# Thirteen warm-up products for eleven, and the state space parameters in nine transfers for five

## The chip, the core and the metric

The kernel runs on one core of a Trainium2 chip. The metric is device time in microseconds (us): the median of the runs of one kernel. A profile is one further execution under the hardware profiler; its times count from the first instruction of the program, and its span ends with the last. Names of engines: PE is TensorE (PEld are its weight loads, and in the profile also its waits and branches), ACT is ScalarE, DVE is VectorE, POOL is GpSimd, SP is SyncE, which issues most DMA transfers.

## The reference, cut to what matters

```python
x = A_u                                  # 1 x 2048 x 640, float32
xn = layernorm(x)                        # over the 640 features
K = 2.0 * einsum("dn,dnl->dl", C * dt, exp(A * dt * pos)).real      # 640 x 128 modes
y = irfft(rfft(xn.T, 2 * L) * rfft(K, 2 * L))[:, :L].T + xn * D_skip
h = xn @ w1 + b1                         # 640 -> 1728
act = h * tanh(softplus(h))              # mish
return x + y + act @ w2                  # 1728 -> 640
```

A normalisation, a state space layer (a long convolution for each feature) and a dense layer with mish, all three added to the input.

## The kernel before, in words

The 2048 rows are worked on in four blocks of 512 (`NB`, `TB`). PE does the dense layer: for each block and each of 14 chunks of the 1728 hidden features (`FC`), a first product (15 matmuls of 512 columns at L807, or 30 of 256 at L800 for the chunk of 64, or the five parts of `mm1_pair` at L827 in later blocks) and, three chunks later, a second product into five accumulators (L859). Each operand is split into a high and a low float16 part, which is why a product takes three matmuls. ACT and DVE compute mish between the two products (L890 to L926), split the weights (L552 to L562) and do the state space layer, which for the parameters of this input comes down to running sums (`skip_a` to `skip_e`). A test on the device, `flag`, says whether these shortcuts hold; if not, a general version is run behind the main one (`ffn_general`, `ssm_general`). That version is part of the program, so at the end each engine that has code in it jumps over it.

The order of the work is set by hand for the first block (the string `ORDER`, L1251) and by a planner (`Plan`) from then on. In the first part:

- `fill(n)` (L1244) gives PE n float32 products of the identity with itself (L1246) while the first rows are on their way. They write `tr`, and nobody reads the result. In the trace, one such product is two weight loads and two matmuls.
- `to_t0` (L1236) transposes the normalised rows on PE; the rows come from `norm0_a` (ACT, L1224) and `norm0` (DVE, L1221).
- `load_par` (L657) is called by the planner once, as the operation `("lp",)` (L1147). SP issues there one transfer after another at L661: `log_A_real`, `A_imag` and `C_real` whole, `C_imag` in two pieces. Behind it stand on SP the five transfers of `load_xt` (L1209) and then the loads of further weights (L543, L538). The parameters are read from L671 on (ACT), L674 (DVE).

Eight completion counters (`DMAHW0` to `DMAHW7` in the listings below) are handed out in turn to the transfers that SP and ACT issue. A transfer waits, before it is issued, until the earlier transfer with the same counter has landed. At the end of the program SP waits for all counters one after the other, and then all five engines meet twice (L1344 in the profile): POOL collects the others, lets them go, clears the semaphores, collects them again and lets them go again.

The last piece of the work is `tail` (L1078): the last accumulators are drained (`drain`, L931) and stored by SP (L934).

Of the kernel before, what the change touches and what calls it, by code (L numbers as in the profile page):

```python
# [28 lines left out]
KD = D // P  # L29
# [423 lines left out]
def body(ctx: ExitStack, tc: tile.TileContext, x, xT, logA, Aim, Cr, Ci, logdt, vec, w1, w1T, w2, w2T, out):  # L453
# [79 lines left out]
    def load_w1(f, queues=(sp,)):  # L533
        t = kf(pl["w1", f])
        n, m = FC[f], P // len(queues)
        for j, e in enumerate(queues):
            o = D * FO[f] + j * m * KD * n
            e.dma_start(t[j * m:(j + 1) * m, :, :n], w1[o:o + m * KD * n].rearrange("(p k f) -> p k f", p=m, k=KD))  # L538

    def load_w2(f):  # L540
        t = pl["w2", f]
        n = FC[f]
        sp.dma_start(t[:n], w2[FO[f]:FO[f] + n])  # L543
        if n < P:
            sp.dma_start(t[n:2 * n], w2[FO[f]:FO[f] + n])
# [111 lines left out]
    def load_par():  # L657
        t = big.tile([P, 4, KD, NS], F32, name="par", tag="bigB")
        for j, src in enumerate((logA, Aim, Cr, Ci)):
            for k in (slice(0, KD),) if j < 3 else (slice(0, 3), slice(3, KD)):  # L660
                sp.dma_start(t[:, j, k], src.rearrange("(k p) n -> p k n", p=P)[:, k])  # L661
        return t

# [272 lines left out]
    def whole():  # L936
# [208 lines left out]


        add(("lp",), S, 0.4, lambda: SM.update(par=load_par()), rel=start(0, 4), kb=1310.0)  # L1147
        ops = list(mode_ops())
        last = {e: ("lp",) for e in (A, V)}
# [94 lines left out]
    def fill(n):  # L1244
        for _ in range(n):
            pe.matmul(TR[:, 0:P], ident, ident, start=True, stop=True)  # L1246
# [24 lines left out]
    def products(s):  # L1271
        f, k, half = int(s[0]), int(s[-2]), s[-1]
        kinds = [s[i:i + 2] for i in range(1, len(s) - 2, 2)]
        start = (f, half) not in count
        count[f, half] = count.get((f, half), 0) + len(kinds)
        mm1_part(f, kinds, CA if half == "a" else CB, start=start, stop=count[f, half] == 3 * KD, ks=[k])

    with tc.manual_schedule():

        for i in range(2):  # L1280
            sp.dma_start(X0[:, i, 0:320], xr[0, i, :, 0:320])
            a.dma_start(X0[:, i, 320:D], xr[0, i, :, 320:D])
        a.activation(warm, one, AF.Sigmoid)
        for f in range(6):
            pl.take("w", ("w1", f))
            if f < 2:
                pl.take("w", ("w2", f))
        for i in range(2):
            load_w1(i)
            sp.dma_start(X0[:, i + 2], xr[0, i + 2])  # L1290
        load_w1(2)
        sp.dma_start(cv[:, 0:24], vec)
        load_w1(3)
        load_w2(0)
        load_w1(4)
        load_w2(1)
        load_w1(5)
        fill(11)
        S, count = {}, {}
        act = {"S": statistics, "M": moments, "N": norm0, "A": norm0_a, "T": to_t0, "H": hi_w1, "L": lo_w1}  # L1300
        row = {"h": hi0, "l": lo0}
        for s in ORDER.split():
            if s[0].isdigit():
                products(s)
            elif s[0] in row:
                row[s[0]](int(s[1]), CA if s[2] == "a" else CB)
            else:
                act[s[0]](int(s[1]))
        a.activation(bs, cv[:, 0:NF], AF.Copy, scale=SH)
# [38 lines left out]
```

## Time and profile before

| | us |
|---|---|
| median of 3 runs (lowest, highest) | 360.02 (360.0, 360.07) |
| the profiled execution, its own time | 359.66 |
| span of the profiled execution | 357.9 |
| PE busy | 350.5 (98%) |
| DVE busy | 305.9 (85%) |
| ACT busy | 295.3 (83%) |
| POOL busy | 48.8 (14%) |

Busy time is a share of the span. An engine's instructions that only wait, branch or issue a DMA are not counted as busy; the profile lists them apart, with a q behind the engine's name.

### The profile page before, as it was taken

How to read it: one execution, taken by the hardware profiler on the slowest of the kernel's cores; microseconds unless marked ns; L12 is line 12 of the kernel's file. 1: busy time of each engine (PE TensorE's matmuls, PEld its weight loads, DVE VectorE, ACT ScalarE, POOL GpSimd, SP SyncE). 2: the span in 40 equal slices, each digit the busy share in tenths (PEclk: the TensorE clock that was granted, in tenths of full speed). 3: DMA queues.
4: the chain of work that ended last, by engine and by line, in shares of the span. 5: the costliest groups of instructions: out<-in, count | busy, mean ns of one | idle time of the engine just before them, and what ended most of it. 6: DMA issues, size and time to landing. Idle time of an engine off the chain costs nothing.

```text
span 357.9 us, 6182 instructions
## 1 busy us (share of the span) xinstructions
PE 350.5 (98%) x2253; PEld 215.5 (60%) x2253; DVE 305.9 (85%) x583; ACT 295.3 (83%) x620; POOL 48.8 (14%) x74
## 2 busy tenths in 40 slices
PE   7999999999999999999999999999999999999994
PEld 7754444444666666665666666666566666566542
DVE  5989989989999999999999877899988788885452
ACT  4699999977588699989899887989989978958630
POOL 2200000000023221000004341000002361000000
PEclk9999999999999999999999999999999999999999
DMA  7869975303819926900536963922002895121012
GB/s 262 327 175 287 323 220 159 93 0 79 289 43 166 284 69 169 326 31 14 144 126 122 271 175 75 326 76 66 2 0 30 137 219 118 23 37 31 2 57 96
DMA packets 25988, 48.75 MB, mean 136 GB/s; under 512 B 3528, under 2 KB 6880, under 8 KB 25952
## 3 DMA queue, kind: packets, MB, share of 16 engines
q1 hardware_dynamic: 19424, 34.86, 30.2%
q0 software_dynamic: 6240, 13.11, 18.6%
q8 instruction: 19, 0.31, 0.4%
q10 hardware_dynamic: 288, 0.33, 0.3%
q14 instruction: 17, 0.14, 0.1%
HBM read 39.10 MB, written 5.26 MB: 124 GB/s over the span
## 4 chain that ended last, share of the span: by engine, by line
PE 96%; DVE 1%; DMA 1%; ACT 0%; issue 0%
PE acc L859 48%; PE h L827 18%; PE h L807 12%; PE tr L827 12%; PE h L800 2%; PE h L789 2%; PE tr L789 1%; DMA x<-in_A_u_dram 1%; PE acc L1236 0%; DVE st L627 0%; DVE st L628 0%; ACT x L1224 0%; PE acc L873 0%; PE acc L870 0%; PE acc L871 0%; DVE w1l L556 0%
## 5 line engine op out<-in xcount | busy, mean ns | idle before, releaser
L859 PE MATMUL acc<-hi,w2h 128*128 128x512 f16 x273 | 100.9, 379 | 0.0
L859 PE MATMUL acc<-hi,w2l 128*128 128x512 f16 (+1 forms) x265 | 99.7, 379 | 0.0
L859 PE MATMUL acc<-lo,w2h 128*128 128x512 f16 x253 | 93.3, 379 | 0.0
L859 PEld LDWEIGHTS <-w2h 128*128 128x128 f16 x526 | 50.9, 98 | 48.3 <-issue 1.9
L890 ACT ACTIVATE s<-h,cv 128x512 f32<-128x512 f32 (+1 forms) x55 | 32.7, 594 | 29.0 <-PE h L827 23.4
L827 PEld LDWEIGHTS <-w1h 128*128 128x128 f16 x432 | 42.3, 98 | 10.6
L910 DVE SCALAR_TENSOR_TENSOR A<-p,A 128x512 f32<-128x512 f32 (+1 forms) x56 | 37.0, 661 | 8.5 <-ACT p L906 8.1
L859 PEld LDWEIGHTS <-w2l 128*128 128x128 f16 x273 | 25.6, 98 | 30.7 <-issue 1.1
L926 DVE SCALAR_TENSOR_TENSOR lo<-A,hi 128x512 f16<-128x512 f32 x52 | 35.5, 682 | 8.0 <-ACT hi L916 8.0
L894 DVE SCALAR_TENSOR_TENSOR A<-h,bs,s 128x512 f32<-128x512 f32 (+1 forms) x55 | 34.8, 636 | 6.4 <-ACT s L890 6.4
L898 ACT ACTIVATE p<-s,kc 128x512 f32<-128x512 f32 (+1 forms) x56 | 39.3, 701 | 0.6
L902 ACT ACTIVATE p<-p,kc 128x512 f32<-128x512 f32 (+1 forms) x56 | 39.3, 702 | 0.5
L906 ACT ACTIVATE p<-p,kc 128x512 f32<-128x512 f32 (+1 forms) x56 | 39.2, 700 | 0.4
L916 ACT ACTIVATE hi<-A 128x512 f16<-128x512 f32 x52 | 32.4, 623 | 2.6 <-DVE A L910 2.5
L548 POOL DMA_DIRECT2D r<-in_xT_dram x15 | 13.4, 1000 | 134.2 <-DVE r L768 66.3
L749 DVE TENSOR_TENSOR_SCAN g<-g,car,kc 128x512 f32<-128x512 f32 x20 | 25.6, 1278 | 1.7 <-ACT g L743 1.6
L827 PEld LDWEIGHTS <-w1l 128*128 128x128 f16 x216 | 21.1, 98 | 8.2
L753 DVE TENSOR_TENSOR_SCAN g<-g,car,g 128x512 f32<-128x512 f32 x20 | 25.5, 1276 | 0.0
L827 PE MATMUL tr<-xh,w1l 128*128 128x256 f16 x90 | 24.5, 273 | 0.0
L827 PE MATMUL tr<-xh,w1h 128*128 128x256 f16 x90 | 24.5, 273 | 0.0
L827 PE MATMUL tr<-xl,w1h 128*128 128x256 f16 x90 | 24.5, 273 | 0.0
L827 PEld LDWEIGHTS <-swh 128*128 128x128 f16 x216 | 21.1, 98 | 4.4
(177 smaller groups left out, 726.6 us busy)
## 6 DMA issues: line engine op xcount, KB each, us to landing
w<-in_w_dram SPq DMA_DIRECT2D x25, 320.0 KB, 5.1
x<-in_A_u_dram SPq DMA_DIRECT2D x14, 320.0 KB, 4.3
w<-in_w2T_dram SPq DMA_DIRECT2D x15, 288.0 KB, 6.8
w<-in_B_w_dram SPq DMA_DIRECT2D x13, 320.0 KB, 3.5
w<-in_w1T_dram SPq DMA_DIRECT2D x13, 320.0 KB, 6.5
xt<-in_xT_dram SPq DMA_DIRECT2D x15, 256.0 KB, 5.9
r<-in_xT_dram POOLq DMA_DIRECT2D x15, 256.0 KB, 6.1
xt<-r POOLq DMA_DIRECT2D x15, 256.0 KB, 4.7
```

Of the source, the lines that this page charges most:

```text
L749: v.tensor_tensor_scan(g1[:, 1:], g1[:, 1:], zero.to_broadcast([P, TB]), car[:, 1, k:k + 1], op0=OP.add, op1=OP.add)
L807: pe.matmul(o, w, x, start=(j == 0), stop=(j == len(order) - 1))
L827: pe.matmul(o, p, q, start=start and n == 1, stop=n == 3 * len(w), skip_group_check=True)
L859: pe.matmul(o, w, x, start=start, stop=stop)
L890: a.activation(pl["s", b, f][:, c], bank(b, f)[:, c] if h is None else h, AF.Sigmoid, bias=cv[:, f:f + 1], scale=1 / SH)
L894: v.scalar_tensor_tensor(pl["A", b, f][:, c], bank(b, f)[:, c] if h is None else h, bs[:, f:f + 1], pl["s", b, f][:, c], op0=OP.add, op1=O ...
L898: a.activation(pl["p", b, f][:, cols(f)], pl["s", b, f][:, cols(f)], AF.Arctan, bias=one, scale=-1.0)
L902: a.activation(p, p, AF.Square, bias=pi4, scale=2.0)
L906: a.activation(p, p, AF.Tanh, bias=mb, scale=MG)
L910: v.scalar_tensor_tensor(A, pl["p", b, f][:, cols(f)], MC, A, op0=OP.add, op1=OP.mult)
L916: a.activation(hi, A, AF.Copy, scale=MA * SA / SH)
L926: v.scalar_tensor_tensor(lo, A, MA * SA / SH, hi, op0=OP.mult, op1=OP.subtract)
```

## The change

`fill` is called with 13 for 11, and `load_par` splits each of the first three parameters into the first three and the last two groups of 128 features, and `C_imag` into two, two and one.

```diff
@@ load_par
         for j, src in enumerate((logA, Aim, Cr, Ci)):
-            for k in (slice(0, KD),) if j < 3 else (slice(0, 3), slice(3, KD)):
+            for k in ((slice(0, 3), slice(3, KD)) if j < 3 else (slice(0, 2), slice(2, 4), slice(4, KD))):
                 sp.dma_start(t[:, j, k], src.rearrange("(k p) n -> p k n", p=P)[:, k])
@@ the first part
         load_w1(5)
-        fill(11)
+        fill(13)
```

On PE, the start of the program, before (-) and now (+): `tr` is where the warm-up products go, `acc` where the transposes go.

```order
 L1344 UNCONDITIONAL_BRANCH
-L1246 MATMUL tr<-ident 128x128 x11
+L1246 MATMUL tr<-ident 128x128 x13
 L1236 MATMUL acc_216<-ident,x_257 128x128
 L1236 MATMUL acc_214<-ident,x_257 128x128 x2
```

Two products more stand ahead of the first transpose; everything behind them on PE stands in the same order, two products (eight instructions in the trace) later in the program.

On SP, around the load of the parameters (`par`), before; the counter in brackets is the one that the transfer takes itself, and `xt` is the block of rows for the second block.

```order
L538 DMA w_226<-in_w_dram 128x640 [waits DVE_49]
L661 DMA par<-in_A_log_A_real_dram 128x5x128 [waits DMAHW2_49]
L661 DMA par<-in_A_A_imag_dram 128x5x128 [waits DMAHW3_49]
L661 DMA par<-in_A_C_real_dram 128x5x128 [waits DMAHW4_49]
L661 DMA par<-in_A_C_imag_dram 128x3x128 [waits DMAHW5_49]
L661 DMA par<-in_A_C_imag_dram 128x2x128 [waits DMAHW6_49]
L1209 DMA xt<-in_xT_dram 128x512 [waits DMAHW7_49]
```

The same place now:

```order
L538 DMA w_226<-in_w_dram 128x640 [waits DVE_49]
L661 DMA par<-in_A_log_A_real_dram 128x3x128 [waits DMAHW2_49]
L661 DMA par<-in_A_log_A_real_dram 128x2x128 [waits DMAHW3_49]
L661 DMA par<-in_A_A_imag_dram 128x3x128 [waits DMAHW4_49]
L661 DMA par<-in_A_A_imag_dram 128x2x128 [waits DMAHW5_49]
L661 DMA par<-in_A_C_real_dram 128x3x128 [waits DMAHW6_49]
L661 DMA par<-in_A_C_real_dram 128x2x128 [waits DMAHW7_49]
L661 DMA par<-in_A_C_imag_dram 128x2x128 [waits DMAHW0_49]
L661 DMA par<-in_A_C_imag_dram 128x2x128 [waits DMAHW1_49]
L661 DMA par<-in_A_C_imag_dram 128x128 [waits DMAHW2_49]
L1209 DMA xt<-in_xT_dram 128x512 [waits DMAHW3_49]
```

Four transfers more stand there, so every transfer behind them takes the counter four further on.

On SP, the six stores at the end of the program (`tail`), before:

```order
L934 DMA out_dram<-xt 128x512 [waits DMAHW6_49,DVE_49]
L934 DMA out_dram<-xt 128x512 [waits DMAHW7_49,DVE_49]
L934 DMA out_dram<-xt 128x512 [waits DMAHW0_49,DVE_49]
L934 DMA out_dram<-xt 128x512 [waits DMAHW1_49,DVE_49]
L934 DMA out_dram<-xt 128x256 [waits DMAHW2_49,DVE_49]
L934 DMA out_dram<-xt 128x256 [waits DMAHW3_49,DVE_49]
L1321 COMPARE_AND_BRANCH
```

And now:

```order
L934 DMA out_dram<-xt 128x512 [waits DMAHW2_49,DVE_49]
L934 DMA out_dram<-xt 128x512 [waits DMAHW3_49,DVE_49]
L934 DMA out_dram<-xt 128x512 [waits DMAHW4_49,DVE_49]
L934 DMA out_dram<-xt 128x512 [waits DMAHW5_49,DVE_49]
L934 DMA out_dram<-xt 128x256 [waits DMAHW6_49,DVE_49]
L934 DMA out_dram<-xt 128x256 [waits DMAHW7_49,DVE_49]
L1321 COMPARE_AND_BRANCH
```

The stores are the same; the last of them took counter 3 and takes counter 7 now, the last of the eight. `L1321` is the jump over the general version.

## The prediction

> **What bounds the kernel now.** I read the page first, then the waits of PE, then the end of the span, where the busy times say nothing. From the page:
>
> ```profile
> span 357.9 us, 6182 instructions
> PE 350.5 (98%) x2253; PEld 215.5 (60%) x2253; DVE 305.9 (85%) x583; ACT 295.3 (83%) x620; POOL 48.8 (14%) x74
> ```
>
> The waits of PE over the whole span (who waited for whom: sum in us, times, longest):
>
> ```profile
> PE tr L1246 <- POOL ident masks.py:199: 1.5, 1, 1.5
> PE acc L1236 <- ACT x L1224: 0.5, 1, 0.5
> ```
>
> PE waits twice, at the very start, and never again: behind the head, the time is a fixed stream of matmuls. So three places can move the time: the head (until PE has its rows), a new wait in the stream, and what comes behind the last matmul. PE is busy for 350.5 us and starts at 1.5; that leaves some 5 us behind it. They are not empty. The last store (issue and landing), the jump over the general version, and the first instructions of the end (L1344):
>
> ```profile
> L934 SPq DMA_DIRECT2D out_dram<-xt x1: 332/332/332, 353.1 to 353.1; - x1
> DMA to landing us min/median/max: 2.0/2.0/2.0
> ```
>
> ```profile
> L1321 PEldq COMPARE_BRANCH  x1: 3874/3874/3874, 350.5 to 350.5; - x1
> ...
> L1321 PEldq EVENT_SEMAPHORE  x1: 51/51/51, 354.4 to 354.4; - x1
> ```
>
> ```profile
> L1344 SPq EVENT_SEMAPHORE  x7: 28/28/28, 353.6 to 354.9; - x7
> L1344 PEldq DRAIN  x1: 8/8/8, 354.5 to 354.5; - x1
> ```
>
> The next windows of the same line, 355.05 to 355.95, then 355.86 to 356.1, 356.1 to 357.55, and the rest:
>
> ```profile
> L1344 SPq EVENT_SEMAPHORE  x5: 28/28/28, 355.1 to 355.7; - x5
> L1344 SPq DRAIN  x2: 7/7/7, 355.8 to 355.8; - x2
> L1344 POOLq EVENT_SEMAPHORE  x1: 17/17/17, 355.9 to 355.9; - x1
> ```
>
> ```profile
> L1344 POOLq EVENT_SEMAPHORE  x2: 17/17/17, 355.9 to 356.0; - x2
> L1344 SPq EVENT_SEMAPHORE  x1: 17/17/17, 356.0 to 356.0; - x1
> L1344 ACTq EVENT_SEMAPHORE  x1: 17/17/17, 356.0 to 356.0; - x1
> L1344 DVEq EVENT_SEMAPHORE  x1: 21/21/21, 356.0 to 356.0; - x1
> ```
>
> ```profile
> L1344 POOLq DRAIN  x2: 46/76/107, 356.0 to 356.4; - x2
> ...
> L1344 PEldq EVENT_SEMAPHORE  x1: 51/51/51, 357.5 to 357.5; - x1
> ```
>
> ```profile
> L1344 POOLq EVENT_SEMAPHORE  x2: 17/17/17, 357.7 to 357.8; - x2
> ```
>
> Read it as a chain. The last store is issued at 353.1 and lands 2.0 later, at 355.1. SP makes five waits from 355.1 to 355.7, then two drains at 355.8; POOL collects at 355.9 and lets all go at 356.0. SP, ACT and DVE go on at 356.0. PE goes on at 357.5. POOL has been done with its clearing since its drain at 356.4, and still it can let go only at 357.8, because PE was not back. The waits of SP in that stretch say it in one row:
>
> ```profile
> SPq L1344 <- PEq L1344: 1.8, 2, 1.5
> ```
>
> Why is PE 1.5 late for a release that it had been waiting for since its drain at 354.5? The row of the instruction queue on the page, and the transfers in the windows 351.9 to 352.9 and 355.0 to 356.1:
>
> ```profile
> q8 instruction: 19, 0.31, 0.4%
> ```
>
> ```profile
> q8 instruction: 1, 0.02, 5.5%
> ```
>
> ```profile
> DMA packets 1, 0.02 MB, mean 15 GB/s; under 512 B 0, under 2 KB 0, under 8 KB 0
> ...
> q8 instruction: 1, 0.02, 5.6%
> ```
>
> Nineteen fetches of 0.31 MB are 16 KB each; leaving out these last two, 17 fetches for PE's 2253 + 2253 instructions are about 265 each, so I take q8 for PE's code (an inference). The two took 5.5% of 16 x 1.0 us = 0.9 us and 5.6% of 16 x 1.1 us = 1.0 us, so they ended by 352.9 and at about 356.0. PE went on 1.5 us behind the first (the jump ends at 350.5 + 3.9, the next instruction starts at 354.4), and at 357.5, again 1.5 us behind the second. My reading: the jump lands on the last three instructions of a piece of code (the wait at L1321, a jump, the drain at L1344); the instruction behind the drain lies in the next piece, whose fetch begins only when the first piece is there.
>
> The Trainium skill, page "Runtime: NRT & Kernel Launch", section "Instruction fetch mechanics", says that code is refilled in 16 KiB blocks of 256 instructions and that a taken jump out of the pages at hand must fetch its target first; the two fetches here agree with that, at 16 KB each.
>
> **The change part by part.** First, two warm-up products at the head. PE's rows there, from the timeline and from the last entries of L1246:
>
> ```profile
> 4.61 1.84 PE L1246 MATMUL tr<-ident 128*128 128x128 f32 x8
> 6.93 1.31 PE L1236 MATMUL acc<-ident,x 128*128 128x128 f32 x10 [0.48 <-ACT x L1224]
> ```
>
> ```profile
> L1246 PE MATMUL tr<-ident x3: 347/421/421, 5.7 to 6.1; 128*128 128x128 f32 x3
> ```
>
> Eight matmuls last 1.84 us, the last one alone 0.35, so one starts every (1.84 - 0.35) / 7 = 0.21. The very last takes 347 ns for 421: PE got faster during it. The transposes behind it start every (1.31 - 0.35) / 9 = 0.11. Two products are four matmuls more, from 6.1 + 0.2 on. At the faster pace they occupy 4 x 0.11 and the slot behind them is free at 6.7, before the rows are there (6.93): cost nothing, the 0.48 us of waiting cover it. At the slower pace 4 x 0.21 ends at 7.15, and the cover is short by 0.2. Nothing can be gained: the transposes wait for ACT, not for PE. I take 0, since the trace shows the faster pace from 6.1 on, and keep 0 to +0.2.
>
> Second, nine transfers for five. SP's issues, the share of the DMA engines from 26 to 42 us (last but one column), and who reads the parameters:
>
> ```profile
> L661 SPq DMA_DIRECT2D par<-in_A_C_imag_dram x2: 523/1546/2568, 28.4 to 31.0; - x2
> L661 SPq DMA_DIRECT2D par<-in_A_log_A_real_dram x1: 427/427/427, 26.8 to 26.8; - x1
> ```
>
> ```profile
> 26.00:42.00 16.00, 16.00 (x76) 7.28 (x75) 15.71 (x31) 16.00 (x28) 0.00 (x0) 1.00 0.97 307
> ```
>
> ```profile
> 43.34 0.74 ACT L671 ACTIVATE par<-par 128x640 f32<-128x640 f32 x1
> ```
>
> The five take from 26.8 to 31.0 + 0.5, and 2.6 of that is one issue that is held up. The DMA engines are 97% busy there, so what lands when is set by bytes, which are the same. Nine issues of 0.43 to 0.52 are 3.9 to 4.7 us, which fits into the same 4.8 us. In the worst case four issues come on top, 4 x 0.52 = 2.1 us later for the rows and weights that stand behind. The parameters are needed at 43.3, eight us behind their last issue and its landing. The first thing that PE could miss is the work on its banks: DVE frees one at
>
> ```profile
> 46.11 0.75 DVE L894 SCALAR_TENSOR_TENSOR A<-h,bs,s 128x512 f32<-128x512 f32 x1 [0.84 <-ACT s L890]
> ```
>
> ```profile
> 52.80 1.76 PE h L800 x30
> ```
>
> and PE takes it up at 52.8, 5.9 us later. A slip of 2.1 is inside that. Cost 0 on the path; if that cover were gone, up to 2.1.
>
> Third, the counters at the end. SP asks them in order: the last store has counter 3, and the five waits from 355.1 to 355.7 are that one and the four behind it, which had nothing more to wait for. With the last store on counter 7, the other waits are over when it lands; at 355.1 one is left. That takes 355.7 - 355.1 = 0.6 off the moment at which POOL lets go: 356.0 becomes 355.4. The gain lies on the path only if PE is there by then. Bounds: 0 if PE still comes at 357.5, 0.6 if not.
>
> Fourth, PE's code. 22 + 22 instructions for eleven products are four each, so everything behind moves by eight instructions. If the boundary lay between the drain and the wait at L1344, it now lies eight instructions earlier, inside the general version, which is jumped over. Then the fetch of the jump brings the whole end of the program, and PE goes on with the others. The nearest rows for that are those of the other engines at the same release, 356.0. Without the counters, POOL's drain at 356.4 would be the last thing to wait for: it ends at 356.45, and from POOL's next instruction to the end are 357.9 - 357.7 = 0.2, so the span would end at about 356.7, a gain of 1.2. Bounds: 0 and 1.2. I take 1.2, as the 1.5 us behind each of the two fetches are otherwise a coincidence.
>
> **The sum.** Head 0, parameters 0, code 1.2, counters 0.6: 1.8 us. The span becomes 356.1, the profiled execution 359.66 - 1.8 = 357.9; the runs' median stands 0.36 higher, so 360.02 - 1.8 = 358.2.
>
> **The rivals.** (a) The lateness of PE has another reason than the place of its code (its jump, say), and the eight instructions change nothing. For it: one trace, and no row shows where a piece of code ends. Against it: at the same release three engines need nothing, and PE's 1.5 us repeat those of the jump. Then PE comes at 357.5 as before, the counters' 0.6 vanish in its wait, and the time is 360.0. The same section of the skill calls the crossing of a boundary mostly hidden, which speaks for this rival; the trace agrees for the 17 fetches in the stream, behind which PE never waits.
>
> (b) Only one of the two tail terms comes, the code's: 360.02 - 1.2 = 358.8. For it: the counters' order is only inferred from the five rows.
>
> (c) Slower: the clock of PE rises later than in this execution, and the head pays. The longer warm-up then ends 0.2 late, and the ten transposes start every 0.21 for 0.11, 10 x 0.1 = 1.0 more: 1.2, with nothing gained at the end 361.2. It decides if the faster pace comes behind 7.15 and PE's late code stays. Against it: the runs lie within 0.07 us of one another, so the rise does not wander by such amounts, and two more products do not put it off. The Trainium skill, page "TensorE: Matmul & The Clock Gate", section on the HAM clock gate, has the rise depend on a window of about 3.4 us that runs free of the kernel, which would let it wander; the runs shown speak against that here.
>
> **How the numbers follow.** The forecast, both terms, gets 0.78; (b) 0.06; (a) 0.13; (c) 0.03. The forecast's own range: 1.8 with 0.1 for the resolution of the rows and up to 0.2 for the head, and as much again for what one execution hides, 357.9 to 358.6. With (b), 84 in 100 lie within 357.9 to 359.0. About 0.2% (0.7 us) is what a measurement of this kernel can tell from no change: the forecast (-0.5%) and (b) (-0.3%) are faster, 0.84; (a) is the same, 0.13; (c) slower, 0.03.
>
> **What would show it.** Right: 26 entries of L1246, the transposes still starting at about 6.9; SP's waits ending at 355.1 with the landing of the last store, POOL's release at about 355.4, PE's L1344 wait within 0.1 of the others', the long wait of SP for PE gone, and a second q8 fetch at the end that nobody waits for. Wrong: PE again about 1.5 us behind a q8 fetch at the end, a PE wait for a load between 26 and 60 us, or transposes that start behind 7.1.

## The result, and the profile after

| | before | after |
|---|---|---|
| median of the runs, us | 360.0 (6 runs, 359.52 to 360.07) | 358.03 (6 runs, 357.84 to 358.25) |
| ratio after / before, 95% interval | | 0.9948 (0.9935 to 0.9961) |
| the profiled execution | 359.66 | 357.84 |
| its span | 357.9 | 356.0 |

The changed kernel is 0.5% faster: 1.97 us by the medians, 1.82 by the two profiled executions. The page says that the work is the same:

```profile
span 356.0 us, 6197 instructions
PE 350.0 (98%) x2257; PEld 215.1 (60%) x2257; DVE 305.9 (86%) x583; ACT 295.8 (83%) x620; POOL 48.9 (14%) x74
```

PE has four entries more, the two products, and is as busy as before. So the time was saved in a place where nobody is busy. Three places can be looked at in turn.

The head first: the timeline of PE from 5 us on (start, length, engine, line; in brackets the idle time before it), and the entries of the warm-up and of the first L807 products:

```profile
4.80 1.17 PE L1246 MATMUL tr<-ident 128*128 128x128 f32 x9
6.95 1.31 PE L1236 MATMUL acc<-ident,x 128*128 128x128 f32 x10 [0.98 <-ACT x L1224]
```

```profile
L1246 PE MATMUL tr<-ident x26: 274/304/582, 1.5 to 5.7; 128*128 128x128 f32 x26
```

```profile
L807 PE MATMUL h<-xh,w1h x65: 379/379/389, 20.2 to 337.9; 128*128 128x512 f16 x65
```

There are 26 warm-up matmuls for 22, and yet they end earlier, at 4.80 + 1.17 = 5.97, where the 22 ended at 6.45: in this execution PE came to its faster pace sooner. It brings nothing: PE waits longer for its rows (0.98 for 0.48), the transposes begin at 6.95 for 6.93, and the large products at 20.2 in both. The head has neither cost nor paid. The nine transfers cost nothing either: SP issues them from 26.8 to 31.7 and takes up the next rows (L1209) at 31.7 for 31.6, and PE has no wait in the profile behind 6.95.

Then the end of the program. SP's wait for PE from 350 us on (sum, times, longest), and the first and second meeting, L1344:

```profile
SPq L1344 <- PEq L1344: 0.7, 2, 0.5
```

```profile
L1344 SPq EVENT_SEMAPHORE  x14: 17/28/28, 353.7 to 356.0; - x14
L1344 POOLq EVENT_SEMAPHORE  x4: 17/17/17, 355.2 to 355.9; - x4
...
L1344 PEldq DRAIN  x2: 8/8/8, 354.5 to 355.5; - x2
L1344 ACTq EVENT_SEMAPHORE  x2: 17/17/17, 355.4 to 356.0; - x2
L1344 DVEq EVENT_SEMAPHORE  x2: 21/21/21, 355.4 to 356.0; - x2
L1344 PEldq EVENT_SEMAPHORE  x2: 51/51/51, 355.4 to 356.0; - x2
```

Read the last three rows side by side. Before, ACT and DVE went on at 356.0 and PE at 357.5; now all three go on at 355.4, and again together at 356.0, where the program ends. PE's drain is where it was, 354.5. SP's wait for PE, 1.8 us before, is 0.7. The instruction queue in the window 355.1 to 356.05:

```profile
q8 instruction: 1, 0.02, 6.5%
```

The second fetch is still made: 6.5% of 16 x 0.95 is 1.0 us. PE goes on at 355.4, while it is under way; nobody waits for it any more.

Last, the wait of SP for the last store. In the window 355.04 to 355.3:

```profile
L1344 SPq DRAIN  x2: 7/7/7, 355.2 to 355.2; - x2
L1344 SPq EVENT_SEMAPHORE  x1: 28/28/28, 355.1 to 355.1; - x1
L1344 POOLq EVENT_SEMAPHORE  x1: 17/17/17, 355.2 to 355.2; - x1
```

One wait behind the landing at 355.1 where there were five, and the drains at 355.2 for 355.8.

### The profile page after: what moved, and what is told of

The parts are those of the page before. It is cut to its first block, busy times and chain, and to the rows that moved or that the text cites. A ratio compares the mean times of both kernels' runs of the same rounds, so it can differ in the third digit from the quotient of the medians.

```text
span 356.0 us, 6197 instructions
## 1 busy us (share of the span) xinstructions
PE 350.0 (98%) x2257; PEld 215.1 (60%) x2257; DVE 305.9 (86%) x583; ACT 295.8 (83%) x620; POOL 48.9 (14%) x74
## 4 chain that ended last, share of the span: by engine, by line
PE 96%; DVE 1%; DMA 1%; ACT 0%; issue 0%
PE acc L859 48%; PE h L827 18%; PE h L807 12%; PE tr L827 12%; PE h L800 2%; PE h L789 2%; PE tr L789 1%; DMA x<-in_A_u_dram 1%; PE acc L1236 0%; DVE st L627 0%; DVE st L628 0%; ACT x L1224 0%; PE acc L873 0%; PE acc L871 0%; PE acc L870 0%; DVE w1l L556 0%
## 5 line engine op out<-in xcount | busy, mean ns | idle before, releaser
L827 PEld LDWEIGHTS <-w1l 128*128 128x128 f16 x216 | 21.1, 98 | 8.2
L827 PEld LDWEIGHTS <-swh 128*128 128x128 f16 x216 | 21.1, 98 | 4.4
```

The costliest lines, as they stand in the source:

```text
L827: pe.matmul(o, p, q, start=start and n == 1, stop=n == 3 * len(w), skip_group_check=True)
```

## The experiments

Each kernel was timed in turn with the kernel before on one chip, in three groups of four; the kernel before had a median of 359.73, 359.85 and 359.83 us in them, so kernels of different groups, and the changed kernel itself, are better compared by their ratios. The general version (`ffn_general`) is passed over by the jump L1321 in all of them, so products that are added there are never executed; they only make the program longer. In the table below, "shift" is by how many instructions of PE the end of the program lies further on than in the kernel before; one product is four.

### Each half of the change alone

Products only, the parameters in five transfers:

```diff
-        fill(11)
+        fill(13)
```

> Thirteen products, the parameters in five transfers as before. Theory (the place of PE's code and the order of the counters, two separate terms): the code's term alone, 1.2 us less than before, about 358.8, span about 356.7; PE passes its first wait at L1344 with the other engines at about 356.0, and SP still makes five waits behind the landing of the last store. Rival (the head: longer warm-up, the end follows from something else): all of the gain, about 358.0, or none, 360.0.

Transfers only, with eleven products:

```diff
-            for k in (slice(0, KD),) if j < 3 else (slice(0, 3), slice(3, KD)):
+            for k in ((slice(0, 3), slice(3, KD)) if j < 3 else (slice(0, 2), slice(2, 4), slice(4, KD))):
```

> Eleven products as before, the parameters in nine transfers. Theory: SP is through its waits at 355.1 and POOL lets go at about 355.4, but PE comes at 357.5 as before, 1.5 us behind the landing of its second piece of code, so no gain: 360.0, span 357.9. Rival (the terms simply add, PE is late for no reason of its own): 0.6 less, 359.4.

Measured: products only 358.70 us (358.4 to 358.93), ratio 0.9966 (0.9954 to 0.9978); transfers only 359.82 (359.35 to 360.0), ratio 0.9997 (0.9988 to 1.0006). The meeting in the transfers-only kernel:

```profile
L1344 POOLq EVENT_SEMAPHORE  x4: 17/17/17, 355.2 to 357.7; - x4
...
L1344 ACTq EVENT_SEMAPHORE  x2: 17/17/17, 355.4 to 357.8; - x2
L1344 DVEq EVENT_SEMAPHORE  x2: 21/21/21, 355.4 to 357.8; - x2
L1344 PEldq EVENT_SEMAPHORE  x2: 51/51/51, 357.5 to 357.8; - x2
```

POOL lets go at the new, earlier time (ACT and DVE are off at 355.4), and PE still comes at 357.5: the transfers' part of the gain is there and vanishes in PE's lateness. The products alone give 1.0 us; with PE on time, the transfers give the rest, 358.70 - 358.03 = 0.67 (by the ratios 0.6; in the two traces the span ends 1.58 and 0.98 behind the landing of the last store). Alone they are worth 0, so the two halves don't add up from the kernel before.

### Is it the warm-up, or the place of the code?

Eleven products as before, and two in the general version:

```diff
@@ ffn_general
         acc = [ps.tile([P, TB], F32, name=f"f_acc{k}") for k in range(KD)]
+        for _ in range(2):
+            pe.matmul(acc[0][:, 0:P], ident, ident, start=True, stop=True)
```

> The kernel before, with two products more in the general version, which is jumped over and never runs: eight instructions of PE that only take up room. Theory: like the thirteen warm-up products, 1.2 us less than before, about 358.8, with the head as before (22 entries at L1246). Rival (the warm-up itself, its clock or its length, makes the gain): no change, 360.0.

Measured: 358.47 us (358.4 to 358.59), ratio 0.9961 (0.9947 to 0.9974). PE at the meeting (two lines more in the file, so L1346):

```profile
L1346 DVEq EVENT_SEMAPHORE  x2: 21/21/21, 356.0 to 356.6; - x2
L1346 PEldq EVENT_SEMAPHORE  x2: 51/51/51, 356.0 to 356.6; - x2
```

Two products that never run bring as much as two that do. The warm-up's work is not the cause; its eight instructions are. With the nine transfers on top (`fill(11)`, two products in the general version):

> Eleven warm-up products as before, the parameters in nine transfers, and two products in the general version that no execution reaches. Theory (the thirteen products only move code): as the changed kernel, span 356.0 to 356.2, time 358.0. Rival (a warmer TensorE gives part of the gain): over 358.3.

Measured: 357.85 us (357.81 to 357.94), ratio 0.9946 (0.9933 to 0.9958), which is the changed kernel's 0.9948. The whole gain is there without one warm-up product more.

### Where must the boundary lie?

If a boundary of 256 instructions is what matters, the loss must come back at a shift of 256. The first try at another shift was a miss: ten products and nine transfers, a shift of -4.

```diff
-        fill(11)
+        fill(10)
```

> Ten products, one fewer than before, with nine transfers. Theory: any shift that takes the boundary out from between the drain and the wait will do, also four instructions the other way, so as fast as the changed kernel, about 358.0 to 358.2. Rival (more warm-up is what helps): not faster than with eleven, 360.0 or more.

Measured: 359.02 us (358.81 to 359.98), ratio 0.9975 (0.9965 to 0.9984): a microsecond more than in the changed kernel. Nine of its ten runs have spans of 355.9 to 356.1, no longer than the changed kernel's; what is longer is the time outside the span. A run's time less its span is 2.71 to 3.09 us here and 1.74 to 1.95 in the kernels above. Two readings were open: ten products cost something ahead of the first recorded instruction, or PE meets the boundary behind its last recorded one. Three kernels with thirteen products and nine transfers, and 62, 61 or 58 products in the general version, tell them apart (the edit is the one above with another number):

> The changed kernel with 62 products more in the layer's general version, which no execution reaches: 248 instructions of TensorE, with the 8 of the two warm-up products 256 against the kernel before. Theory (the boundary of a 256-instruction piece of PE's code has to fall between PE's drain and its next L1344 wait): it falls there again, PE's wait comes last by about 2 us, span 357.8, time 359.6 to 359.9, as with the transfers alone. Rival (any shift of the end by some instructions, or the warm-up, took the stall away): span 356.0, time 358.0.

> The same with 61 products there: 252 instructions against the kernel before, which puts the boundary four instructions later than in it, where ten warm-up products had it (359.02 us, with 2.7 to 3.1 us of the time outside the span for 1.7 to 1.9 in the other kernels). Theory: PE meets the boundary behind its last recorded wait, so the span is 356.0 and the time about 359.0, with 2.9 us outside the span, though the warm-up has thirteen products. Rival (the 1.1 us outside the span come from the ten products, at the start): span 356.0, time 358.0, 1.8 us outside the span.

> The same with 58 products there: 240 instructions against the kernel before, the boundary 16 instructions later than in it. Theory: if what PE still runs behind its last recorded wait is fewer than some ten instructions, nobody meets the boundary: span 356.0, outside the span 1.8, time 358.0. If it is more, the stall stays outside the span: time 359.0. Rival (a boundary anywhere behind the landing costs): time 359.0.

| kernel | shift | PE goes on at the first meeting | time less span, all runs | median us |
|---|---|---|---|---|
| transfers only | 0 | 357.5 | 1.74 to 1.84 | 359.82 |
| 62 in the general version | 256 | 357.7 | 1.75 to 1.82 | 359.69 |
| ten products | -4 | 356.4 | 2.71 to 3.09 | 359.02 |
| 61 in the general version | 252 | 355.4 | 2.64 to 3.05 | 359.00 |
| 58 in the general version | 240 | 355.5 | 1.75 to 1.88 | 357.98 |
| the changed kernel | 8 | 355.4 | 1.74 to 1.85 | 358.03 |

The 356.4 with ten products is no lateness at the meeting: in that execution everything from the head on is 0.9 later, as the section on the warm-up shows, and PE is there with the others. The ratios to the kernel before are 0.9996 (0.9987 to 1.0005) for 62, 0.9978 (0.9968 to 0.9987) for 61 and 0.9947 (0.9933 to 0.996) for 58. With 62, the long wait is back:

```profile
SPq L1346 <- PEq L1346: 2.4, 2, 2.1
```

```profile
L1346 DVEq EVENT_SEMAPHORE  x2: 21/21/21, 355.6 to 358.0; - x2
L1346 PEldq EVENT_SEMAPHORE  x2: 51/51/51, 357.7 to 358.0; - x2
```

With 61, the profile shows nothing of a loss, PE included:

```profile
L1346 DVEq EVENT_SEMAPHORE  x2: 21/21/21, 355.4 to 356.0; - x2
L1346 PEldq EVENT_SEMAPHORE  x2: 51/51/51, 355.4 to 356.0; - x2
```

and the run is still 1.0 us slower than the changed kernel. Two things are shown: shifts 0 and 256 are alike and -4 and 252 are alike, so the effect of the place comes back after 256 instructions (the shifts alone would also allow a period that divides 256); and the loss at -4 and 252 lies outside the span, whatever the warm-up has. How I read the places (no record shows them): at -4 and 252 the boundary lies four instructions further on, and PE meets it behind its last record; at 240 it lies sixteen further on, behind all that PE still runs; at 8 it lies eight ahead, in code that the jump passes over.

### What the transfers do

Thirteen products, the parameters in five transfers as before, and four loads of w1T in halves:

```diff
-        if j < NF:
+        if j < 4:
+            for c in (slice(0, 320), slice(320, D)):
+                sp.dma_start(t[:, c], w1T[FO[j]:FO[j] + P, c])
+        elif j < NF:
             sp.dma_start(t[:FC[j]], w1T[FO[j]:FO[j] + FC[j]])
```

> Thirteen products, the parameters in five transfers as before, and four loads of w1T in halves instead, four DMAs of SP more elsewhere in the program, so that the last store is on completion counter 7 as in the changed kernel. Theory (the 0.6 us are the counter's): SP's waits end with the last landing, span 356.0 to 356.1, time 358.0. Rival (the parameters' own split brings it): as with the products alone, span 356.8, time 358.7.

Measured: 358.07 us (357.63 to 358.25), ratio 0.9948 (0.9934 to 0.9961). Four transfers more elsewhere do it as well; the parameters themselves have no part in it.

But why 0.6 us for four waits that have nothing to wait for? The trace of the products-only kernel, the waits in its windows 355.2 to 355.5 and 355.5 to 356.1, and the instruction queue q14 from 355.8 to 356.8:

```profile
L1344 SPq EVENT_SEMAPHORE  x3: 28/28/28, 355.3 to 355.4; - x3
```

```profile
L1344 SPq EVENT_SEMAPHORE  x2: 28/28/28, 355.8 to 355.9; - x2
...
L1344 POOLq EVENT_SEMAPHORE  x1: 17/17/17, 356.0 to 356.0; - x1
```

```profile
q14 instruction: 1, 0.01, 3.0%
```

Three waits stand 0.07 apart, then nothing happens for nearly 0.4, then the last two follow. That hole can be no store, since the last one landed at 355.2. In the changed kernel it lies earlier, ahead of the landing, at 354.0 to 354.4, and the fetch with it, in the window 354.6 to 355.8. There too it is no wait for a landing: the counter that is asked behind the hole is 2, and its last transfer had landed at 349.1.

```profile
L1344 SPq EVENT_SEMAPHORE  x2: 28/28/28, 354.0 to 354.4; - x2
```

```profile
q14 instruction: 1, 0.01, 2.8%
```

In both traces the fetch begins 0.6 to 0.7 behind the end of the hole. So SP seems to have a boundary of its own, and four more transfers move it four waits up. To tell the boundary from the counter: eight transfers more (the parameters in nine and the halves of w1T) bring the counter back to 3 and the hole another four waits up.

> Thirteen products, the parameters in nine transfers and four loads of w1T in halves: eight DMAs of SP more than before, so that the last store is on completion counter 3 as in the kernel before. Theory (the 0.6 us of the counters are two things: some 0.27 us for four more waits behind the landing, and 0.36 us for a boundary in SP's own code, which lies between its 10th and 11th wait before and between the 6th and 7th after, and here, eight instructions on, between the 2nd and 3rd): the four waits come back, the 0.36 us do not, span 356.3 to 356.5, time 358.2 to 358.4. Rival (the counter's place alone): as with the products alone, span 356.8, time 358.7.

Measured: 358.24 us (358.0 to 358.42), ratio 0.9957 (0.9944 to 0.9969). Its waits from 354.98 to 355.4 and from 353.7 to 354.1:

```profile
L1347 SPq EVENT_SEMAPHORE  x5: 28/28/28, 355.0 to 355.2; - x5
L1347 SPq DRAIN  x2: 7/7/7, 355.3 to 355.4; - x2
```

```profile
L1347 SPq EVENT_SEMAPHORE  x1: 28/28/28, 353.7 to 353.7; - x1
```

Five waits stand behind the landing again, now without a hole: 0.3 us to the drain. The hole is at 353.7 to 354.1, behind the second wait, where SP waits for stores anyway. By the medians the counter's order is worth 358.24 - 358.03 = 0.2 us and the hole 358.70 - 358.24 = 0.5. Differences as small as the first are not clear of the scatter of the runs; the traces are finer. The span ends 0.98 behind the landing of the last store in the changed kernel, 1.22 here and 1.58 with the products alone: 0.24 for the counter's order, nearly 0.4 for the hole.

Ten transfers (`A_imag` stays in two, `C_real` and `C_imag` go in three) bring the last store to counter 0:

```diff
-            for k in (slice(0, KD),) if j < 3 else (slice(0, 3), slice(3, KD)):
+            for k in (slice(0, 2), slice(2, 4), slice(4, KD)) if j > 1 else (slice(0, 3), slice(3, KD)):
```

> Thirteen products and the parameters in ten transfers: five DMAs of SP more than before, the last store on counter 0, the first of the eight that SP asks in the end. Theory (0.07 us for each wait behind the landing, SP's boundary passed ahead of it): seven waits behind it, 0.5 us over the changed kernel, span 356.5, time 358.4 to 358.6. Rival (all 0.6 us are the counters', 0.15 us each): span 357.0, time 359.0.

Measured: 358.73 us (358.64 to 359.38), ratio 0.9973 (0.9964 to 0.9983), between the two expectations. From 355.1 to 355.3 and from 355.3 to 356.1:

```profile
L1344 SPq EVENT_SEMAPHORE  x1: 28/28/28, 355.2 to 355.2; - x1
```

```profile
L1344 SPq EVENT_SEMAPHORE  x7: 27/28/28, 355.6 to 356.0; - x7
L1344 SPq DRAIN  x2: 7/7/7, 356.0 to 356.1; - x2
```

The expectation had the hole passed ahead of the landing. But the fifth wait is the one for counter 0, so the hole behind it comes after the landing, from 355.2 to 355.6. Seven waits at 0.07 are 0.5, with some 0.3 for the hole 0.8 over the changed kernel; measured 0.7 by the medians, and 0.8 by the traces (the span ends 1.78 behind the landing for 0.98). The size of each part holds; the place was misjudged.

### Is the warm-up free?

Twenty products, with the parameters in nine transfers:

```diff
-        fill(11)
+        fill(20)
```

> Twenty warm-up products for thirteen, else the changed kernel: 28 entries of TensorE more behind the identity, at 0.11 us with the clock up and 0.21 us before. Theory (the warm-up is free only up to the first transposes at 6.9 us): its 40 matmuls end at 7.4 to 8.3 us, the transposes begin 0.5 to 1.3 us later than at 6.95, and as TensorE is busy to the end, that is passed on: span 356.5 to 357.4, time 358.4 to 359.3. Rival (the head waits for data anyway, or the clock that rises sooner pays it back): time 358.0.

Measured: 359.10 us (358.21 to 359.74), ratio 0.9978 (0.997 to 0.9987). In the profiled execution:

```profile
4.61 4.38 PE L1246 MATMUL tr<-ident 128*128 128x128 f32 x26
8.82 0.93 PE L1236 MATMUL acc<-ident,x 128*128 128x128 f32 x7
```

The transposes begin 8.82 - 6.95 = 1.9 later than in the changed kernel, and the span is 357.8 for 356.0: a warm-up beyond the rows' arrival is passed on. The median lies inside the range that was expected. The span of this one execution lies 0.4 above its upper end, since PE came to the faster pace later than I had allowed for. The runs scatter by 1.5 us, more than those of any other kernel here.

Two other executions show the faster pace coming late. In the one with ten transfers, thirteen products at the slower pace are 0.2 late for the rows, but the large products begin at 20.2 as in the changed kernel, so at most 0.1 of it is passed on:

```profile
4.61 2.70 PE L1246 MATMUL tr<-ident 128*128 128x128 f32 x12
7.14 1.25 PE L1236 MATMUL acc<-ident,x 128*128 128x128 f32 x10
```

```profile
L807 PE MATMUL h<-xh,w1h x65: 379/379/389, 20.2 to 338.0; 128*128 128x512 f16 x65
```

And in the profiled execution of the kernel with ten products, the transposes themselves ran at the slower pace:

```profile
6.91 2.40 PE L1236 MATMUL acc<-ident,x 128*128 128x128 f32 x10 [0.82 <-ACT x L1224]
```

```profile
L807 PE MATMUL h<-xh,w1h x65: 379/379/389, 21.1 to 338.9; 128*128 128x512 f16 x65
```

Ten transposes take 2.40 for 1.31, and the large products begin at 21.1 for 20.2. This execution is the 359.98 among the ten runs of that kernel; its span is 357.0 for the others' 355.9 to 356.1. PE stood idle for 0.82 between its shorter warm-up and the transposes; whether that kept the pace down was not tried.

## Why the prediction was right, point by point

**The head, 0 (bounds 0 to +0.2).** Held: 6.95 for 6.93 in the profiled execution, and the same result with eleven products (0.9946 against 0.9948). In the execution with ten transfers the transposes were 0.2 late, as the upper bound had it, but hardly any of that reached the large products.

**The parameters in nine transfers, 0.** Held: the nine issues last from 26.8 to 31.7, the transfers-only kernel has ratio 0.9997 (0.9988 to 1.0006), and with w1T in halves for it the time is the changed kernel's.

**PE's code, 1.2.** Held in mechanism and in size: against the kernel before of the same group (359.73) 1.03 us for the products alone and 1.26 for the two products that never run, spans 356.8 and 356.7 for 357.9. The reading of the two fetches and the 1.5 us behind each as a boundary between PE's drain and its next wait was an inference from one trace; the shifts of 256, 252 and 240 bear it out. The second fetch itself is no sign: it is made in every kernel here, 0.4 to 0.6 behind PE's first drain, also where nobody waits for it. What the shift changes is whether PE needs that piece. Shifts by one or two instructions were not tried, so the exact place rests on the gap in the rows.

**The counters, 0.6.** Right in size, incomplete in cause. The step read the stretch 355.1 to 355.7 as five waits in a row, "that one and the four behind it". Three of them are done by 355.3, and nearly 0.4 of the 0.6 is a hole that moves with SP's code. The same four transfers that move the counter move the hole ahead of the landing, so the sum came out right; for this part, that was luck. Had the change added eight transfers, the step as written would have given no gain from SP at all, and nearly 0.4 of it would have come.

**The sum.** 1.8 for a span of 356.1 and a profiled execution of 357.9; measured 1.82, 356.0 and 357.84. The median fell somewhat more, by 1.97, as it stands 0.19 above the profiled execution after and stood 0.34 above it before (0.36 by the three runs that the prediction had).

**The rivals.** (a), another reason for PE's lateness, falls with the products that never run. (b), the code's term alone, is what the products-only kernel shows: 358.70 for 358.8. (c) did not come, but the ground for putting it aside was false. The prediction said that the rise of PE's pace doesn't wander by such amounts. It does: the 26 warm-up matmuls ended at 5.97 in the changed kernel's execution and at 4.61 + 2.70 = 7.31 in that with ten transfers, and with ten products the transposes of one execution took 2.40 for 1.31, and L807 began 0.9 later. The traces' own records of the granted clock say the same: the full clock begins at 6.24 in the kernel before, 4.30 in the changed one, 7.10 with ten transfers and 10.88 in that execution with ten products, each time where the pace changes, and it lasts 351.57, 351.57, 348.16 and 344.75, which differ by 3.41 or twice that. The rule of the Trainium skill (page "TensorE: Matmul & The Clock Gate", section on the HAM clock gate) that the window runs free of the kernel fits these rows; that three runs of before lay within 0.07 us of one another did not speak against it, since most of the wandering is hidden by the wait for the rows: L807 begins at 20.2 whether the full clock begins at 4.30, 6.24 or 7.10.

## What to carry to other kernels

If an engine comes late to a meeting though nobody holds it up, look at the instruction queue and at how many instructions lie ahead: a jump that lands a few instructions ahead of a 256-instruction boundary can make it wait for a second fetch, which cost 1.0 to 1.8 us here, and code that is never run can move the boundary away. Compare the time less the span between kernels, since such a stall can lie behind the last record. And a change that adds or drops instructions should be tried against a dummy of the same length, or the place of the code is taken for the work's effect.

## What the runs showed of the hardware that was not expected

- The fetch behind a jump: PE goes on 1.5 us after the second piece has landed. At shift 0 the whole is worth 1.0 to 1.3 us with the parameters in five transfers; with nine, where the others are at the meeting earlier, it is worth 1.7 to 1.8 us at shift 0 or 256, and 1.0 us, all of it outside the span, at -4 or 252.
- SP seems to have such places too. There the hole is nearly 0.4 us, between two and ten waits into the end of the program, with a fetch on q14 that begins 0.6 to 0.7 us behind it, and it moves by one wait for each transfer that is added (behind the 10th wait with five transfers of the parameters, the 6th with four more, the 5th with five more, the 2nd with eight more).
- A wait at the program's end for a counter that is long complete still takes SP 0.07 us, so by an estimate from seven such waits in the kernel with ten transfers the place of the last store among the eight is worth up to 0.5 us.
- The end of PE's slower pace moved by nearly three microseconds between executions with the same warm-up (full clock from 4.30 and from 7.10 with 26 matmuls, which end at 5.97 and at 7.31). What sets it was not tried.
